# Attention with pooled keys and a mixture of adapters: the second query group by cast and transpose DMAs, and chunks that enter the adapters in another order

## The chip, the cores and the metric

The kernel runs on one core of a Trainium2 chip. The metric is the device time of one execution in microseconds (us). The core's engines work side by side, each through its own instructions in order: TensorE (PE in the profile; its weight loads are PEld), VectorE (DVE), ScalarE (ACT), GpSimd (POOL) and SyncE (SP), which here only issues DMAs. Matmuls write to PSUM[...].

## What is computed

Four batches of 12288 queries of 128 channels attend to 768 keys each. The keys, which are also the values, are the means of 4x4 patches of `kv`, times `w_sr`. Each row of the result then goes through the two best of eight low-rank adapters, weighted by a softmax over the two logits, and is added to itself.

```python
kv_pool = kv.reshape(B, H // r, r, W // r, r, C).mean(axis=(2, 4))
kv_flat = kv_pool.reshape(B, -1, C) @ w_sr
k = v = kv_flat
s = scale * (q @ k.transpose(0, 2, 1))
...
out = (a @ v)                      # a = softmax(s); these are the rows x
...
logits = x @ w_gate                # 8 adapters, the two best are kept
...
z = x[mask] @ A[e]                 # 128 -> 16
delta[mask] += w[mask, k, None] * (z @ B[e])
return (x + delta)
```

## The kernel before

A *chunk* is 512 queries: 24 chunks a batch, 96 in all. Four chunks are a *query group* `g` (2048 queries), whose transposed form `qT[g]` is what the scores need. Nearly all groups are made by two DMAs: a cast to bf16 into DRAM, issued by GpSimd, and a transposing DMA into SBUF, issued by SyncE. The first two groups are instead loaded as f32, transposed on TensorE and copied by ScalarE:

```python
def cast_q(g):
    t = qdram.tile([GT, C], BF16, tag=f"q{g}", name=f"qbf{g}")
    keep(nc.gpsimd.dma_start(t, q[g // NG, (g % NG) * GT:(g % NG + 1) * GT]))
    q_bf[g] = t

def load_qT(g):
    t = qpool.tile([P, GT], BF16, tag="qT", name="qT")
    keep(nc.sync.dma_start(t.rearrange("c (j p) -> c j p", p=P),
                           q_bf[g].rearrange("(p j) c -> p (j c)", p=P), transpose=True))
    qT[g] = t
...
def turn_q(g, m, engine):
    ...
    for i in range(S):
        mm(ps[:, i], q_f[g][:, m * S + i], id_f, is_transpose=True,
           start=(i == 0), stop=(i == S - 1))
    ...
        keep(nc.scalar.copy(o, ps))
...
load_q(0, 0, GC * S)
for h in range(3):
    for r in range(4):
        for x in range(2):
            load_kv(0, h, r, x)
for m in range(GC):
    load_q(1, m * S, m * S + S)
```

The scores of a chunk come in three parts of 256 keys, each two matmuls of 512 columns and one exponential. They share two PSUM buffers. The weighted sum over the values needs 24 matmuls of 137 columns (128 channels, 8 logits of the adapters, and the sum of the weights) into a single PSUM buffer, which `normalize` empties:

```python
def scores(k, r):
    ...
    ps = ps_s.tile([P, 2, T], FP32, tag="sg", name="sg")        # 2 buffers
    for i in range(2):
        mm(ps[:, i], kfT[b][:, 2 * r + i], rhs, start=True, stop=True)
    keep(nc.scalar.activation(em[k][:, 2 * r:2 * r + 2], ps, AF.Exp, bias=0.0, scale=scale))

def normalize(k):
    keep(nc.vector.reciprocal(ri, acc[k][:, :, VC]))
    ...
    keep(nc.vector.tensor_tensor(x, acc[k][:, :, 0:VC],
                                 ri.unsqueeze(2).broadcast_to([P, S, VC]), op=ALU.mult))
```

The adapters of a chunk `k` then take, in later steps: `top` (VectorE finds the sorted logits), `route` (differences, a tanh on ScalarE, the gate weights `gw`; on VectorE for the first groups, on GpSimd for the others), `transposes` (of `x` and of the gated hidden rows `hg`, four matmuls each, with one copy out of PSUM), `down` (x times A), `gate` (VectorE), `up` (times B), and `finish` (the sum with `x` on VectorE, and the output DMA). Chunks are routed in groups of the sizes

```python
sizes = [1, 1, 2] + [GC] * (NCHUNK // GC - 5) + [2] * 4 + [1] * 8
```

The main loop has one step for each `k` from 4 on, and `enter` says which chunks enter the adapters in it (`kx`; `kh` is what entered in the step before, `ku` the one before that). `att` names the chunks whose weighted sum is taken in a step: one, but two in the steps 6, 7 and 8.

```python
late = const.tile([P, 1], FP32)
keep(nc.gpsimd.tensor_copy(late, q_f[1][:, GC * S - 1, 0:1]))
for g in range(2, 4):
    cast_q(g)
...
turn_q(1, 0, nc.scalar)
...
for k in range(NCHUNK):
    done = normed[first[k] + size[k] - 1]
    two = size[k] < GC and k % 4 == 0 and len(enter.get(e, [])) < 2
    e = max(e if two else e + 1, done + 1)
    enter.setdefault(e, []).append(k)
...
for k in range(LA, NCHUNK):
    ...
    scores(k, 0)
    while later:
        later.pop(0)()                  # tanh and gate weights of a route
    for n in kn:
        normalize(n)
    ...
    for x_, h_ in pairs[:1]:
        transposes(x_, h_)
    if k + 1 in range(GC + 1, 2 * GC):
        turn_q(1, (k + 1) % GC, nc.scalar)
    scores(k, 1)
    for u_ in ku:
        up(u_)
        finish(u_)
    ...
    scores(k, 2)
    for x_ in kx[:1]:
        down(x_)
        gate(x_)
    ...
            attend(a_, s)
    for x_, h_ in pairs[1:]:
        transposes(x_, h_)
    for x_ in kx[1:]:
        down(x_)
        gate(x_)
    ku = kh
    kh = kx
    if b + 1 < B and 10 <= i < 21:
        ...                             # GpSimd sums patches of the next batch's keys
```

After the loop a tail, written out by hand, finishes the last four chunks.

Of the kernel before, what the change touches and what calls it, by code (L numbers as in the profile page):

```python
# [10 lines left out]
FP32 = mybir.dt.float32  # L11
# [9 lines left out]
def kernel(  # L21
# [104 lines left out]
    for h in range(3):  # L126
        for r in range(4):
            for x in range(2):
                load_kv(0, h, r, x)
    for m in range(GC):  # L130
        load_q(1, m * S, m * S + S)
    b_f = const.tile([P, C], FP32)
    keep(nc.sync.dma_start(b_f, moe_B.rearrange("e r c -> (e r) c")))
    a_f = const.tile([P, P], FP32)
# [131 lines left out]

    sizes = [1, 1, 2] + [GC] * (NCHUNK // GC - 5) + [2] * 4 + [1] * 8
    first, size = {}, {}  # L270
    for n in sizes:
        k0 = len(first)
# [11 lines left out]

    def route(k0):
        n = size[k0] * S
        eng = nc.gpsimd if k0 > 1 else nc.vector
        lg = xg[k0].rearrange("p m s c -> p (m s) c")[:, 0:n, C:VC]
        so = srt[k0].rearrange("p m s e -> p (m s) e")[:, 0:n]

        def over(i):
            d = rpool.tile([P, GC * S, 8], FP32, tag=f"over{i}", name=f"over{i}")[:, 0:n]
            keep(eng.tensor_tensor(  # L293
                d, lg, so[:, :, i].unsqueeze(2).broadcast_to([P, n, 8]), op=ALU.subtract))
            return d

        arg, mask = over(0), over(1)
        keep(eng.tensor_tensor(arg, arg, mask, op=ALU.add))
        keep(eng.tensor_scalar(mask, mask, 0.0, None, op0=ALU.is_ge))


        def rest():
            gates(k0, n, eng, arg, mask)

        if k0 > 3:
            later.append(rest)
        else:
            rest()
# [6 lines left out]
        keep(eng.tensor_tensor(w[:, 0:n], w[:, 0:n], mask, op=ALU.add))  # L315
        gw[k0] = w

    def transposes(kx, kh):

        ps = mtile([P, 2, S, P], BF16, name="tt_ps")  # L320
        if kx is not None:
            xb = xn[kx].bitcast(U16)[:, :, 1::2].bitcast(BF16)
            for s in range(S):
                mm(ps[:, 0, s], xb[:, s, 0:C], id_bf, is_transpose=True,
                   start=(s == 0), stop=(s == S - 1))
        if kh is not None:
            for s in range(S):
                mm(ps[:, 1, s], hg[kh][:, s], id_bf, is_transpose=True,
                   start=(s == 0), stop=(s == S - 1))
        sb = run.tile([P, 2, S, P], BF16, tag="tts", name="tts")  # L330
        lo = 0 if kx is not None else 1
        hi = 2 if kh is not None else 1
        keep(nc.vector.tensor_copy(sb[:, lo:hi], ps[:, lo:hi]))  # L333
        if kx is not None:
            xT[kx] = sb[:, 0]
        if kh is not None:
            hgT[kh] = sb[:, 1]

    def down(k):
        hp[k] = mtile([P, S, P], name="h_ps")  # L340
        for s in range(S):
            mm(hp[k][:, s], xT[k][:, s], a_bf, start=(s == 0), stop=(s == S - 1))
# [44 lines left out]
    rest = []  # L387

    late = const.tile([P, 1], FP32)
    keep(nc.gpsimd.tensor_copy(late, q_f[1][:, GC * S - 1, 0:1]))  # L390
    for g in range(2, 4):
        cast_q(g)
    a_bf = const.tile([P, P], BF16)
    keep(nc.vector.tensor_scalar(a_bf, a_f, 0.5, None, op0=ALU.mult))
    b_bf = const.tile([P, C], BF16)
    keep(nc.vector.tensor_copy(b_bf, b_f))
    turn_q(1, 0, nc.scalar)


    att = {LA: [0], LA + 1: [1], LA + 2: [2, 3], LA + 3: [4, 5], LA + 4: [6, 7]}  # L400
# [3 lines left out]
    for t, ks in att.items():  # L404
        for k in ks:
            normed[k] = t + 1 if k == ks[-1] else t
    enter = {}
    e = 0
    for k in range(NCHUNK):
        done = normed[first[k] + size[k] - 1]  # L410
        two = size[k] < GC and k % 4 == 0 and len(enter.get(e, [])) < 2
        e = max(e if two else e + 1, done + 1)
        enter.setdefault(e, []).append(k)

    sums, rest = [], []
    kh, ku = [], []
    for k in range(LA, NCHUNK):
        b, i = divmod(k, NB)
        ka = att.get(k, [])
# [5 lines left out]
            if 4 <= g + 2 < B * NG and g + 2 not in q_bf:  # L425
                cast_q(g + 2)
        if b + 1 < B:
            if i == 4:
                sums, rest = prepare(b + 1, nc.gpsimd)
            if 4 <= i < 16:  # L430
                h, j = divmod(i - 4, 4)
                load_kv(b + 1, h, j, None)

        def after_norm(kn):
# [9 lines left out]
        scores(k, 0)  # L444
        while later:
            later.pop(0)()
        for n in kn:
            normalize(n)
        pairs = [(kx[j] if j < len(kx) else None, kh[j] if j < len(kh) else None)
                 for j in range(max(len(kx), len(kh)))]  # L450
        for x_, h_ in pairs[:1]:
            transposes(x_, h_)
        if k + 1 in range(GC + 1, 2 * GC):
            turn_q(1, (k + 1) % GC, nc.scalar)
        scores(k, 1)
        for u_ in ku:
            up(u_)
# [11 lines left out]
        for x_ in kx[:1]:  # L469
            down(x_)  # L470
            gate(x_)
        if rest and i in (14, 15, 16, 18, 19, 20, 21, 22, 23):
            rest.pop(0)()
        for a_ in ka[-1:]:
            for s in range(1 if len(ka) == 1 else 0, S):
                attend(a_, s)
        for x_, h_ in pairs[1:]:
            transposes(x_, h_)
        for x_ in kx[1:]:
            down(x_)  # L480
            gate(x_)
        ku = kh
        kh = kx
        if b + 1 < B and 10 <= i < 21:
            h, j = divmod(i - 10, 4)
            for _ in range((4, 3, 1, 0)[j]):
                sums[h].pop(0)()

    K = NCHUNK - 1
    assert kh == [K - 3] and ku == [K - 4], (kh, ku)  # L490
# [92 lines left out]
    gate_part(K - 2, 0, S)  # L583
    add_there(K - 4)

    ri = rpool.tile([P, S], FP32, tag="rinv", name="rinv")
    keep(nc.vector.reciprocal(ri, o95[:, :, VC]))
    xn[K] = xpool.tile([P, GC, S, VC], FP32, tag="xn", name="xn")[:, 0]
    for s in range(2):
        keep(nc.scalar.activation(xn[K][:, s, 0:C], o95[:, s, 0:C], AF.Copy, bias=0.0,  # L590
                                  scale=ri[:, s:s + 1]))
    lg = rpool.tile([P, S, E], FP32, tag="lg", name="lg")
    keep(nc.vector.tensor_tensor(lg, o95[:, :, C:VC], ri.unsqueeze(2).broadcast_to([P, S, E]),
                                 op=ALU.mult))
    keep(nc.vector.tensor_tensor(xn[K][:, 2:S, 0:C], o95[:, 2:S, 0:C],  # L595
                                 ri[:, 2:S].unsqueeze(2).broadcast_to([P, 2, C]), op=ALU.mult))
    tanhs()
    so = rpool.tile([P, S, 8], FP32, tag="so", name="so")
    for s in range(S):
# [15 lines left out]
    fetch(xT, K)  # L615
    th = rpool.tile([P, S, E], FP32, tag="th1", name="th1")
    keep(nc.scalar.activation(th, arg, AF.Tanh, bias=0.0, scale=0.5))
    gate_part(K - 1, 0, S)
    gw[K] = gpool.tile([P, S, E], FP32, tag="gw1", name="gw1")
    keep(nc.vector.scalar_tensor_tensor(gw[K], th, 1.0, mask, op0=ALU.add, op1=ALU.mult))  # L620
    down_into(K, ps_s)
    fetch(hgT, K - 2)
    carry(K - 3)
    add_there(K - 3)
    gate_part(K, 0, 2)
    gate_part(K, 2, S)
    up_into(K - 2, wide(bank(ps_s)))
    turn_h(K - 1, ps_m)
    fetch(hgT, K - 1)
    ps = bank(ps_m).bitcast(BF16).rearrange("p a b -> p (a b)")[:, 0:T].rearrange("p (s c) -> p s c", s=S)  # L630
    hgT[K] = run.tile([P, S, P], BF16, tag="tt1", name="tt1")
    for lo in (0, 2):
        for s in range(lo, lo + 2):
            mm(ps[:, s], hg[K][:, s], id_bf, is_transpose=True, start=(s == lo), stop=(s == lo + 1))
    keep(nc.scalar.copy(hgT[K][:, 0:2], ps[:, 0:2]))
    add_here(K - 2, 0, S, nc.sync)
    keep(nc.vector.tensor_copy(hgT[K][:, 2:S], ps[:, 2:S]))
    up_into(K - 1, bank(ps_m))
    dp[K] = wide(bank(ps_a))
    for lo in (0, 2):  # L640
        for s in range(lo, lo + 2):
            mm(dp[K][:, s], hgT[K][:, s], b_bf, start=(s == lo), stop=(s == lo + 1))
    add_here(K - 1, 0, S, nc.sync)
    add_here(K, 0, 2, nc.scalar)
    add_here(K, 2, S, nc.sync)


# [28 lines left out]
```

The softmax here doesn't subtract the row's maximum and nothing guards it: scores larger than these inputs give would overflow.

## Time and profile before

| | before |
|---|---|
| time, median of 3 runs | 407.59 us (407.49 to 407.65) |
| span in the profile | 405.0 us |
| PE busy | 383.8 us (95%) |
| DVE busy | 324.9 us (80%) |
| ACT busy | 292.2 us (72%) |
| POOL busy | 170.4 us (42%) |
| DMA moved | 76.45 MB, mean 189 GB/s |
| exponential, 128x1024 | 288 of 1023 ns |
| score matmuls, 512 columns | 576, 170.9 us |
| value matmuls, 137 columns | 2280, 171.6 us |
| qT_ps, f32 transposes | 32, 6.1 us |

The busy share of an engine is its time at work over the span. Slices cut the span into 40 equal parts and give a busy share in tenths, a digit a part. A line of a timeline gives start, length, engine, source line, operation, result and source tiles, and how many; in brackets stands the idle time of that engine just before it and what ended it. Names with an arrow read "result from source": `tt_ps<-id_bf,xn` are the transposes of `x`, `sg` are scores, `acc` are weighted sums.

### The profile page before, as it was taken

The numbers are of one execution on the slowest core, as the hardware profiler recorded it, in microseconds if no ns is written. First come the engines' busy times: TensorE is split into PE (matmuls) and PEld (weight loads), VectorE is DVE, ScalarE is ACT, GpSimd is POOL, SyncE is SP. The second block draws the span as 40 slices with busy tenths as digits, with TensorE's granted clock in tenths as the row PEclk, the third lists the DMA queues.
The fourth block names the chain that finished last, engine by engine and source line by source line (L and its number), as shares of the span: only waits on it lengthen the run. The fifth ranks groups of instructions, "written<-read, shape, count | busy, mean of one in ns | idle before, by whom it ended". The sixth has DMA issues, their size and how long they took to land.

```text
span 405.0 us, 11448 instructions
## 1 busy us (share of the span) xinstructions
PE 383.8 (95%) x4589; PEld 307.4 (76%) x4589; DVE 324.9 (80%) x950; ACT 292.2 (72%) x343; POOL 170.4 (42%) x289
## 2 busy tenths in 40 slices
PE   3898899999999999999999999999999999989893
PEld 3656778888888888888888888888888788777682
DVE  2543778888888888889888888889888888888885
ACT  2489468767678778767678778867678778667683
POOL 0010128778512318779411319779411313114342
PEclk9999999999999999999999999999999999999996
DMA  8997577994855999994844999996855765542213
GB/s 305 382 264 243 125 163 210 299 201 123 183 130 108 298 180 337 290 230 126 183 131 107 304 171 321 216 296 151 187 132 114 172 134 92 143 131 102 83 53 133
DMA packets 71318, 76.45 MB, mean 189 GB/s; under 512 B 49920, under 2 KB 50432, under 8 KB 70784
## 3 DMA queue, kind: packets, MB, share of 16 engines
q1 hardware_dynamic: 70128, 63.98, 55.3%
q0 software_dynamic: 704, 11.54, 16.8%
q8 instruction: 36, 0.59, 0.6%
q10 hardware_dynamic: 432, 0.20, 0.2%
q14 instruction: 18, 0.15, 0.1%
HBM read 50.53 MB, written 36.70 MB: 215 GB/s over the span
## 4 chain that ended last, share of the span: by engine, by line
PE 88%; DVE 5%; ACT 2%; DMA 1%; issue 1%; POOL 0%; DVEq 0%; ACTq 0%
PE acc L68 34%; PE sg L68 28%; PE tt_ps L68 9%; PE h_ps L68 5%; PE d_ps L68 5%; PE kpT_ps L68 2%; ACT em L246 2%; DVE xn L263 1%; DMA w_sr_sb<-in_w_sr_dram 1%; PE qT_ps L68 1%; PE v_ps L68 1%; DVE tts L333 1%; PE kfT_ps L68 1%; DVE hg L347 1%; DVE kvr L175 1%
## 5 line engine op out<-in xcount | busy, mean ns | idle before, releaser
L246 ACT ACTIVATE em<-sg 128x1024 f16<-128x1024 f32 x288 | 278.9, 1023 | 91.6 <-PE sg L68 91.4
L68 PE MATMUL sg<-qT,kfT 128*128 128x512 bf16 x576 | 170.9, 378 | 2.7 <-ACT em L246 2.2
L68 PE MATMUL acc<-vx,em 128*128 128x137 f16 x2280 | 171.6, 224 | 1.7 <-DVE xn L263 1.6
L68 PEld LDWEIGHTS <-em 128*128 128x128 f16 x2304 | 149.6, 98 | 4.0 <-DVE xn L263 2.2
L68 PEld LDWEIGHTS <-tts 128*128 128x128 bf16 x740 | 56.4, 98 | 45.8 <-DVE tts L333 2.1
L293 POOL TENSOR_TENSOR over<-xn,srt 128x128 f32<-128x128 f32 (+2 forms) x62 | 21.4, 363 | 157.2 <-DVE srt L281 157.2
L347 DVE TENSOR_TENSOR hg<-h_ps,gw 128x512 bf16<-128x512 f32 x93 | 64.2, 690 | 13.2 <-POOL gw L315 7.5
L263 DVE TENSOR_TENSOR xn<-acc,rinv 128x544 f32<-128x544 f32 x95 | 68.8, 724 | 3.3
L333 DVE COPY tts<-tt_ps 128x1024 bf16<-128x1024 bf16 (+1 forms) x96 | 64.4, 671 | 3.6 <-PE tt_ps L68 3.6
L171 POOL TENSOR_TENSOR kvr<-kvr 128x512 f32<-128x512 f32 x54 | 66.7, 1270 | 0.0
L360 DVE TENSOR_TENSOR osb<-d_ps,xn 128x512 f32<-128x512 f32 x91 | 62.5, 690 | 0.5 <-PE d_ps L68 0.5
L68 PEld LDWEIGHTS <-kfT 128*128 128x128 bf16 x576 | 45.9, 97 | 6.0 <-issue 3.7
L68 PEld LDWEIGHTS <-xn 128*128 128x128 bf16 x384 | 29.3, 98 | 21.9 <-DVE xn L595 0.5
L258 DVE RECIPROCAL rinv<-acc 128x4 f32<-128x4 f32 x95 | 17.2, 181 | 32.7 <-PE acc L68 31.5
L68 PE MATMUL h_ps<-a_bf,tts 128*128 128x128 bf16 x372 | 36.0, 219 | 1.6 <-DVE tts L333 1.6
L68 PE MATMUL d_ps<-b_bf,tts 128*128 128x128 bf16 x364 | 35.2, 219 | 1.3 <-DVE tts L333 1.3
L68 PE MATMUL tt_ps<-id_bf,xn 128*128 128x128 bf16 x372 | 35.9, 219 | 0.0
L68 PE MATMUL tt_ps<-id_bf,hg 128*128 128x128 bf16 x368 | 35.6, 219 | 0.3 <-DVE hg L347 0.3
L281 DVE MAX8 srt<-xn 128x8 f32<-128x8 f32 x380 | 34.2, 153 | 0.2
L314 POOL TENSOR_TENSOR gw<-th,over 128x128 f32<-128x128 f32 (+2 forms) x31 | 12.0, 387 | 37.1 <-ACT th L312 37.0
L68 PEld LDWEIGHTS <-hg 128*128 128x128 bf16 x384 | 25.4, 98 | 0.7 <-DVE hg L347 0.4
L169 POOL TENSOR_TENSOR kvr<-kvr 128x512 f32<-128x512 f32 (+1 forms) x18 | 18.1, 1004 | 0.9
(83 smaller groups left out, 175.4 us busy)
## 6 DMA issues: line engine op xcount, KB each, us to landing
out_dram<-osb SPq DMA_DIRECT2D x95, 256.0 KB, 3.6
kvr<-in_kv_dram SPq DMA_DIRECT2D x36, 512.0 KB, 6.3
qbf<-in_q_dram POOLq DMA_DIRECT2D x22, 512.0 KB, 6.3
kvr<-in_kv_dram SPq DMA_DIRECT2D x24, 256.0 KB, 4.9
qf<-in_q_dram SPq DMA_DIRECT2D x1, 1024.0 KB, 5.0
qf<-in_q_dram SPq DMA_DIRECT2D x4, 256.0 KB, 5.0
qT<-qbf SPq DMA_TRANSPOSE x22, 6.9
out_dram<-osb ACTq DMA_DIRECT2D x1, 128.0 KB, 3.2
```

The costliest lines, as they stand in the source:

```text
L68: return keep(nc.tensor.matmul(*a, **k))
L169: keep(adder.tensor_tensor(u, u, v, op=ALU.add))
L171: keep(adder.tensor_tensor(u[:, lo:hi], u[:, lo:hi], v[:, lo:hi], op=ALU.add))
L246: keep(nc.scalar.activation(em[k][:, 2 * r:2 * r + 2], ps, AF.Exp, bias=0.0, scale=scale))
L258: keep(nc.vector.reciprocal(ri, acc[k][:, :, VC]))
L263: keep(nc.vector.tensor_tensor(x, acc[k][:, :, 0:VC], ri.unsqueeze(2).broadcast_to([P, S, VC]), op=ALU.mult))
L281: keep(nc.vector.max(srt[k0][:, m, s], xn[k][:, s, C:VC]))
L293: keep(eng.tensor_tensor(d, lg, so[:, :, i].unsqueeze(2).broadcast_to([P, n, 8]), op=ALU.subtract))
L314: keep(eng.tensor_tensor(w[:, 0:n], th, mask, op=ALU.mult))
L333: keep(nc.vector.tensor_copy(sb[:, lo:hi], ps[:, lo:hi]))
L347: keep(nc.vector.tensor_tensor(hg[k].rearrange("p s (e r) -> p (s e) r", e=E), hp[k].rearrange("p s (e r) -> p (s e) r", e=E), gw[k0][:, m ...
L360: keep(nc.vector.tensor_tensor(osb, dp[k], xn[k][:, :, 0:C], op=ALU.add))
```

## The change

The second query group is no longer loaded as f32 and transposed on TensorE. It is cast and transposed by DMA, right behind the loads of the first batch's keys: a tiny GpSimd copy that reads the last key load holds the cast until then, and another that reads `qT[1]` holds the casts of the groups 2 and 3 until the transpose has landed. Beside it come the changes of an earlier form, joined with it: chunks are routed one by one at both ends and in pairs between; the chunk that enters in a step is found by readiness, with two in the steps 73 and 75 only; the second transposes of such a step go to ScalarE for the copy, and their down product into the next step; the key loads and sums of the next batches are spread differently over the steps; and in the tail the last chunk is normalized in one operation and gates, transposes and sums of the last two chunks come in halves.

```diff
-    for m in range(GC):
-        load_q(1, m * S, m * S + S)
...
-    sizes = [1, 1, 2] + [GC] * (NCHUNK // GC - 5) + [2] * 4 + [1] * 8
+    sizes = [1] * GC + [2] * (NB * (B - 1) // 2 - 2) + [1] * NB
...
-        eng = nc.gpsimd if k0 > 1 else nc.vector
+        eng = nc.gpsimd if k0 >= GC else nc.vector
...
+        if engine is nc.scalar:
+            keep(nc.scalar.copy(sb[:, lo:hi], ps[:, lo:hi]))
+        else:
+            keep(nc.vector.tensor_copy(sb[:, lo:hi], ps[:, lo:hi]))
...
-    keep(nc.gpsimd.tensor_copy(late, q_f[1][:, GC * S - 1, 0:1]))
+    keep(nc.gpsimd.tensor_copy(late, kvr[0, 2][:, 3, 1, 0:1]))
+    cast_q(1)
+    load_qT(1)
+    late2 = const.tile([P, 1], BF16)
+    keep(nc.gpsimd.tensor_copy(late2, qT[1][:, GT - 1:GT]))
     for g in range(2, 4):
         cast_q(g)
...
-    turn_q(1, 0, nc.scalar)
...
+    ready = {k: normed[first[k] + size[k] - 1] + (k >= GC or k == 2) for k in range(NCHUNK)}
+    enter, t, left = {}, LA, list(range(NCHUNK - 3))
+    while left:
+        can = [k for k in left if ready[k] <= t]
+        enter[t] = can[:2] if t in (NB * (B - 1) + 1, NB * (B - 1) + 3) else can[:1]
+        left = [k for k in left if k not in enter[t]]
+        t += 1
...
-            if i == 4:
+            i0 = 4 if b == 0 else 0
+            if i == i0:
                 sums, rest = prepare(b + 1, nc.gpsimd)
...
+        for x_ in kd:
+            down(x_)
...
-            transposes(x_, h_)
-        if k + 1 in range(GC + 1, 2 * GC):
-            turn_q(1, (k + 1) % GC, nc.scalar)
+            transposes(x_, h_, nc.vector)
+        for x_ in kd:
+            gate(x_)
...
+                if s == S - 1:
+                    for x_, h_ in pairs[1:]:
+                        transposes(x_, h_, nc.scalar)
+                        kd = [x_] if x_ is not None else []
                 attend(a_, s)
...
-        kh = kx
-        if b + 1 < B and 10 <= i < 21:
-            h, j = divmod(i - 10, 4)
-            for _ in range((4, 3, 1, 0)[j]):
-                sums[h].pop(0)()
+        kh = kx[:1] + kdone
+        kdone = kd
+        if b + 1 < B and i % 2 == 0 and (8 if b == 0 else 6) <= i <= 20:
+            for _ in range(4 if b == 0 and i % 4 else 3):
+                sums.pop(0)()
...
-    for s in range(2):
-        keep(nc.scalar.activation(xn[K][:, s, 0:C], o95[:, s, 0:C], AF.Copy, bias=0.0,
-                                  scale=ri[:, s:s + 1]))
...
+    acc[K] = o95
+    normalize(K)
+    lg = xn[K][:, :, C:VC]
...
-    gate_part(K, 0, 2)
-    gate_part(K, 2, S)
+    halves = [(K, 0), (K, 2), (K - 1, 0), (K - 1, 2)]
+    for k, lo in halves:
+        gate_part(k, lo, lo + 2)
```

## The prediction

> **What bounds the kernel now.** I read the page from the top: busy shares, the slices, the chain of waits; then busy time by stretch, which tells where TensorE is not full; then the timeline of the two stretches that stood out.
>
> The slices:
>
> ```profile
> PE   3898899999999999999999999999999999989893
> ACT  2489468767678778767678778867678778667683
> DMA  8997577994855999994844999996855765542213
> ```
>
> TensorE is at 9 nearly everywhere; neither ACT nor the DMA engines stay at their top. The chain of waits is 88% PE. So a gain can only come from TensorE work that disappears, or from the places where TensorE waits. Busy time by stretch finds those (columns: length, then PE, PEld, DVE, ACT, POOL):
>
> ```profile
> 30.00:42.00 12.00, 10.61 (x111) 7.89 (x108) 4.38 (x17) 10.25 (x14) 0.00 (x0) 1.00 0.82 236
> 42.00:54.00 12.00, 10.91 (x136) 8.66 (x136) 8.60 (x35) 6.20 (x9) 2.43 (x7) 1.00 0.59 123
> ...
> 110.00:130.00 20.00, 20.00 (x251) 15.98 (x249) 17.44 (x51) 15.22 (x17) 3.21 (x7) 1.00 0.70 143
> ...
> 330.00:350.00 20.00, 19.48 (x244) 15.56 (x242) 16.62 (x48) 15.11 (x18) 6.34 (x17) 1.00 0.62 143
> 350.00:370.00 20.00, 18.30 (x231) 14.57 (x228) 16.92 (x50) 13.68 (x18) 4.50 (x15) 1.00 0.34 97
> 370.00:384.00 14.00, 12.89 (x165) 10.35 (x163) 11.61 (x32) 9.58 (x13) 4.85 (x21) 1.00 0.24 90
> ```
>
> From 70 to 330 us TensorE is full, and a step of the main loop takes 3.68 us (in the chain its 18 value matmuls start at 120.30, 123.98, 127.66). It idles before 6 us, about 2.5 us in 30 to 54, 0.52 + 1.70 + 1.11 = 3.3 us in 330 to 384, and after 392. The change touches the last three.
>
> The start, where the second query group is made (timeline; start, length):
>
> ```profile
> 25.16 1.26 POOL L79 DMA_DIRECT2D qbf<-in_q_dram  x2
> ...
> 28.98 0.59 PE L68 MATMUL sg<-qT,kfT 128*128 128x512 bf16 x2 [0.33 <-ACT em L246]
> ...
> 29.41 0.60 PE L68 MATMUL qT_ps<-id_f,qf 128*128 128x128 f32 x4
> ...
> 29.84 1.66 PE L68 MATMUL acc<-vx,em 128*128 128x137 f16 x24
> ...
> 30.80 2.45 SPq L84 DMA_TRANSPOSE qT<-qbf  x1
> 31.33 0.59 PE L68 MATMUL sg<-qT,kfT 128*128 128x512 bf16 x2
> ```
>
> 31.33 is the first score of chunk 4, the first to use the second query group. DMA issues in the windows 25.1 to 25.6 and 30.5 to 31 show how long such a cast and such a transpose take when little else runs (5.6 and 4.6 us to landing):
>
> ```profile
> qbf<-in_q_dram POOLq DMA_DIRECT2D x1, 512.0 KB, 5.6
> qT<-qbf SPq DMA_TRANSPOSE x1, 4.6
> ```
>
> The late stretch, one step in which a second chunk enters the adapter:
>
> ```profile
> 347.39 0.39 PE L68 MATMUL tt_ps<-id_bf,xn 128*128 128x128 bf16 x4
> ...
> 347.82 0.42 DVE L333 COPY tts<-tt_ps 128x512 bf16<-128x512 bf16 x1 [0.65 <-PE tt_ps L68]
> ...
> 348.30 0.40 PE L68 MATMUL h_ps<-a_bf,tts 128*128 128x128 bf16 x4 [0.52 <-DVE tts L333]
> ```
>
> TensorE transposes the second chunk, has nothing else in its order, and waits for VectorE's copy.
>
> **What the skill says.** "DMA: Bandwidth & Descriptors", section "SWDGE vs HWDGE vs iDMA": a cast in flight must be issued from GpSimd and a transpose from SP or ACT, so the new path is two DMAs, the second waiting for the first. The trace agrees: the cast issued at 25.16 lands 5.6 us later, at 30.8, where the transpose starts. "PSUM — Partial Sum Buffer", section "Engine vs sequencer instructions": ACT, VectorE and GpSimd queues are strict FIFO and matmuls stay in program order; the wait at 348.30 is such a case, and I use it to follow the new order. "TensorE: Matmul & The Clock Gate", section "Back-to-back issue gap": N/2.4 + 2.5 ns a matmul. A steady step has 6 of 512, 24 of 137 and 16 of 128 columns, 8408 columns and 46 matmuls: estimate 3.62 us, measured 3.68, so I count 0.438 ns a column. "SBUF — State Buffer", section "SBUF: two separate sides": a GpSimd operation that reads SBUF is locked out while VectorE adds two SBUF inputs; VectorE does that from 21.19 to 23.67, so the new gate may start a few tenths late. No number here shows that yet.
>
> **Part by part.**
>
> (1) *Second query group.* Removed: four loads of 256 KB, 16 f32 transposes on TensorE (about 0.5 us per four in the stream, 2.0 us) and four ACT copies of 0.6 us. Added: gate, cast, transpose in series. The old gate fired at 25.04, when the query loads behind the keys had landed. In the DMA packets, the last key packet ends about 3 us before the last query packet, near 22.0. With 0.1 to 0.6 us for gate and issue: cast from about 22.4, landed 28.0, transposed 32.6. TensorE would be ready about 30.75 (31.33 less 0.5 for the absent transposes). So a new wait of about 1.9 us; chunk 4 starts at 32.6 instead of 31.33, 1.3 us later. The third group (cast at 32.8, landed about 38.4, transposed by 43 to 48) is needed only about 20 us after chunk 4, near 52: hidden.
>
> (2) *The first five steps.* Before, chunk 4 to chunk 9 takes 31.33 to 55.95, 24.6 us. The new order makes the first four chunks groups of one, routed on VectorE, and each enters one step earlier, so one chunk more of adapter work (4 x 512 = 2048 columns, 0.9 us) is done by chunk 9. Columns: 5x3072 + 7x3288 + 3584 + 2048 + 1024 = 45032, 19.7 us if full. Waits, with the durations of the page (exponential 0.96 to 1.02, normalize 0.9, route about 1.07 plus gate weights 0.4, gate 0.69): in steps 4 and 5 TensorE runs two PSUM buffers ahead of ACT at most, +1.7; in step 6 VectorE routes chunk 2 and then chunk 1 before it gates chunk 1 (about 3.8 us from the normalize), and the next hidden transpose waits for it, +1.4; in step 7 normalize, route and gate of chunk 3 cost +2.1; step 8, +1.0. Sum 25.9 us, 1.3 more than before. Chunk 9 then starts at 58.5, 2.6 us later.
>
> (3) *Late doubles.* Before, chunks enter six steps behind at first and three at the end: three double steps. From the score starts 343.71, 348.53, 352.76, 357.25 one double takes 4.82 + 4.23 + 4.49 = 13.54 instead of 3x3.68 = 11.04: 2.5 us, of which 0.9 is its work. Three: 7.5 us. After: five steps behind, so two doubles (steps 73 and 75), the second transpose copied by ACT inside the value matmuls and its down product put into the next step. Each keeps 0.9 us of work; for waits I leave 0.7 in all, mostly step 76 where VectorE has two gates and two sums, 3.33 + 1.38 = 4.7 against 4.1 us of TensorE. Two: 2.5 us. Saved 5.0. (This includes the one chunk done earlier in part 2.)
>
> (4) *Middle.* Groups of two instead of four: more small GpSimd operations, TensorE's order per step unchanged: 0 expected.
>
> (5) *Tail.* Before, the last score step ends near 391.6 and the program at 405.0, 13.4 us. Normalizing the last chunk in one VectorE operation lets its transposes go at about 395.2 instead of 395.7; gates and sums come in halves, and the last sums, now ending at 400.70, end about 0.5 earlier. Saved 0.5.
>
> Sum: +2.6 - 5.0 - 0.5 = -2.9; 407.6 - 2.9 = 404.7, rounded to 404.8.
>
> **Rivals.** (A) *The DMA pair takes the place of the transposes and more*: for it, 5.6 + 4.6 us in series and median landings of 6.3 and 6.9 over the whole run; against it, the DMA engines are nearly free then. With the medians chunk 4 starts at about 35.5 and the total is near 407.7. (B) *ACT and VectorE become the bound in the middle*: 34 pairs bring more tanhs, and an ACT held up by a late GpSimd result holds the scores. For it: 3 or 4 key sums of 1.27 us sit before the route on GpSimd; three end about 2.7 us into the odd step, where the logits arrive at 2.8, four end at 3.9 and leave only a tenth before the tanh. Against: ACT is 75 to 80% busy. 0.1 us a pair would be 3.5 us, total about 408. (C) *My waits in the first steps are too high*: ACT loses 2.4 us of copies where it is the bound, and then the start costs nothing: total near 402.5.
>
> **Range and chances.** About 1 us each for the landing, the early waits and the doubles, and a one-sided 1 to 3 us for (B): 402.2 to 408.2. Two per cent is 8.1 us; faster by that means 399.4, more than all TensorE idle that the change can reach in (2), (3) and (5) together. Faster 0.04, same 0.94, slower 0.02.
>
> **What would show it.** A TensorE wait on the DMA transpose near 31 to 33 us of 1 to 3 us; chunk 9 at about 58.5; 20.00 of 20.00 TensorE busy in the middle (less would be rival B); under 1.2 us of idle between 330 and the tail; the last sum 12.9 us or less after the last score step. I am wrong if the query transpose lands before 31 or after 35, if the middle step is not 3.68, or if the doubles still wait for a copy.

## The result, and the profile after

The changed kernel takes 413.31 us (median of four, 410.96 to 422.76) against 407.54 us for the kernel before on the same chip. The ratio is 1.0123, with a 95% interval of 1.008 to 1.0166: a loss of 5 to 6 us in 407 where a gain of 2.9 was forecast, outside the range. The same kernel once more gave 412.5 us and 1.0119 (1.0087 to 1.0151). The first execution profiled took 422.76 us and holds a wait of its own, shown further down, so the profile after is here that of an execution of 409.57 us, the shortest of the eight, span 407.6 against 405.0.

Its page, the slices and the chain of waits:

```profile
PE   3896798999999999999999999999999999999992
...
DMA  8959883992739999987767997862862736653213
...
PE 82%; DMA 6%; DVE 4%; SPq 3%; ACT 2%; POOL 1%; issue 1%; DVEq 0%; ACTq 0%
```

The 8s that stood near the end of TensorE's row are now 9: the late idle is gone, as intended. But the row is lower in slices 4 to 7 (6, 7, 9, 8), about 30 to 70 us. DMA, 1% of the chain before, is 6%.

Busy time by stretch, the same stretches as in the prediction (length, then PE, PEld, DVE, ACT, POOL, clock, DMA share, GB/s):

```profile
30.00:42.00 12.00, 8.35 (x82) 5.46 (x81) 4.30 (x17) 8.26 (x10) 1.57 (x4) 1.00 0.87 175
42.00:54.00 12.00, 9.49 (x127) 7.93 (x125) 9.21 (x43) 4.69 (x8) 0.00 (x0) 1.00 0.92 251
110.00:130.00 20.00, 20.00 (x252) 16.37 (x249) 17.67 (x55) 15.32 (x20) 6.25 (x20) 1.00 0.67 159
330.00:350.00 20.00, 20.00 (x255) 16.31 (x254) 17.02 (x52) 15.88 (x21) 8.95 (x36) 1.00 0.51 144
350.00:370.00 20.00, 20.00 (x251) 16.10 (x250) 17.37 (x49) 16.06 (x23) 8.01 (x32) 1.00 0.69 149
370.00:384.00 14.00, 14.00 (x178) 11.28 (x176) 11.93 (x36) 11.16 (x15) 5.99 (x24) 1.00 0.20 76
```

TensorE idles 3.65 + 2.51 = 6.2 us between 30 and 54, where it idled 2.5. The middle is full, and so is everything from 330 to 384. The loss must lie before 70 us, or in places that these stretches leave out.

The start (timeline: start, length):

```profile
23.01 0.28 POOL L391 COPY late<-kvr 128x1 f32<-128x1 f32 x1 [21.70 <-DMA kvr<-in_kv_dram]
23.23 0.76 POOL L79 DMA_DIRECT2D qbf<-in_q_dram  x1
...
29.02 2.53 SPq L84 DMA_TRANSPOSE qT<-qbf  x1
...
30.17 1.66 PE L68 MATMUL acc<-vx,em 128*128 128x137 f16 x24
...
33.62 1.04 PE L68 MATMUL sg<-qT,kfT 128*128 128x512 bf16 x4 [1.79 <-DMA qT<-qbf]
33.63 0.18 POOL L395 COPY late<-qT 128x1 bf16<-128x1 bf16 x1 [9.65 <-DMA qT<-qbf]
```

Gate at 23.01, cast landed where the transpose starts (29.02), transpose landed at 33.6. TensorE ends its last ready work at 31.83 and waits 1.79 us. Chunk 4 starts at 33.6 instead of 31.3.

I then cut each trace at the first score weight load of a step and took the differences. "Start" is the start of chunk 4, "end" runs from the score start of step 95 to the end of the span; all in us:

| | start | steps 4 to 8 | 9 and 10 | 11 to 71 | 72 to 81 | 82 to 94 | end | span |
|---|---|---|---|---|---|---|---|---|
| before | 31.27 | 24.61 | 7.36 | 232.57 | 36.80 | 55.34 | 17.08 | 405.0 |
| after | 33.61 | 26.42 | 8.91 | 232.62 | 40.79 | 47.84 | 17.40 | 407.6 |
| difference | +2.34 | +1.81 | +1.55 | +0.05 | +3.99 | -7.50 | +0.32 | +2.6 |

This table locates all of the 2.6 us. Two columns were not in the forecast at all (9 and 10, and the sign of the end). It does not yet tell why the other seven executions take 1.4 to 13.2 us more than this one.

### The profile page after: what moved, and what is told of

It is laid out like the page before. It is cut to its first block, busy times and chain, and to the rows that moved or that the text cites. A ratio compares the mean times of both kernels' runs of the same rounds, so it can differ in the third digit from the quotient of the medians.

```text
span 420.7 us, 11578 instructions
## 1 busy us (share of the span) xinstructions
PE 380.1 (90%) x4500; PEld 306.1 (73%) x4573; DVE 327.2 (78%) x957; ACT 295.4 (70%) x370; POOL 197.9 (47%) x447
## 4 chain that ended last, share of the span: by engine, by line
PE 69%; DMA 18%; DVE 5%; SPq 2%; issue 2%; POOL 1%; ACT 1%; DVEq 0%; POOLq 0%; ACTq 0%
PE acc L68 27%; PE sg L68 20%; DMA qT<-qbf 14%; PE tt_ps L68 9%; PE d_ps L68 5%; PE h_ps L68 5%; SPq L98 2%; DMA qbf<-in_q_dram 2%; DMA qf<-in_q_dram 1%; DMA kvr<-in_kv_dram 1%; DVE xn L261 1%; DVE rinv L256 1%; PE v_ps L68 1%; POOL kvr L169 1%; DVE hg L348 1%
## 5 line engine op out<-in xcount | busy, mean ns | idle before, releaser
L68 PE MATMUL sg<-qT,kfT 128*128 128x512 bf16 x503 | 156.9, 383 | 15.0 <-DMA qT<-qbf 13.0
L334 DVE COPY tts<-tt_ps 128x1024 bf16<-128x1024 bf16 (+1 forms) x91 | 62.6, 688 | 18.9 <-PE tt_ps L68 18.9
L291 POOL TENSOR_TENSOR over<-xn,srt 128x64 f32<-128x64 f32 (+1 forms) x114 | 29.7, 281 | 80.6 <-DVE srt L279 80.4
L312 POOL TENSOR_TENSOR gw<-th,over 128x64 f32<-128x64 f32 (+1 forms) x57 | 16.6, 291 | 87.1 <-ACT th L310 87.0
L297 POOL TENSOR_SCALAR over<-over 128x64 f32<-128x64 f32 (+1 forms) x57 | 19.0, 333 | 5.1
```

The lines of the kernel that those rows point to most:

```text
L68: return keep(nc.tensor.matmul(*a, **k))
L291: keep(eng.tensor_tensor(d, lg, so[:, :, i].unsqueeze(2).broadcast_to([P, n, 8]), op=ALU.subtract))
L312: keep(eng.tensor_tensor(w[:, 0:n], th, mask, op=ALU.mult))
```

## The experiments

The first theory after the result (theory T in the expectations) was that the transposes of the query pair land late and that this is what costs. Its rival (M) was that the new order of chunks is slow by itself. The first four experiments showed a part of each and two things more, a stall in step 10 and a spread of the times. For the spread, theory C names the casts that are issued right behind transposes, and rival L the first cast and transpose alone. All experiments are compared with the kernel before on the same chip (407.64 to 407.84 us); intervals are 95%.

### The same kernel again

No edit.

> The changed kernel once more, unchanged, to get a second profile. Theory T (the query transposes by DMA land late): the time is again 411 to 414 us and TensorE again waits 2 to 4 us for the first DMA transpose near 31 to 35 us; the 9 us wait for a transpose near 273 us was one bad landing, and is shorter or gone here. Rival M (the middle itself became slower through the pairs on GpSimd): TensorE shows less than 19.8 of 20 us in most stretches from 70 to 330 us, without any wait on a DMA.

Measured: 412.5 us (409.57 to 420.8), ratio 1.0119 (1.0087 to 1.0151). The loss repeats and so does the spread, of more than 10 us, where the kernel before keeps within 1.3 us. The trace shown above is from here. In its step 10 stands this (timeline):

```profile
60.79 3.72 POOL L169 TENSOR_TENSOR kvr<-kvr 128x512 f32<-128x512 f32 x3
...
64.48 0.31 POOL L312 TENSOR_TENSOR gw<-th,over 128x64 f32<-128x64 f32 x1
...
64.86 0.32 POOL L313 TENSOR_TENSOR gw<-gw,over 128x64 f32<-128x64 f32 x1
...
65.22 0.69 DVE L348 TENSOR_TENSOR hg<-h_ps,gw 128x512 bf16<-128x512 f32 x1 [2.42 <-POOL gw L313]
...
65.97 0.40 PE L68 MATMUL tt_ps<-id_bf,hg 128*128 128x128 bf16 x4 [1.38 <-DVE hg L348]
```

GpSimd sums three patches of the next keys (3.72 us), and only then makes the gate weights of the first pair, whose tanh was ready at 61.95. VectorE waits 2.42 us for them, TensorE 1.38 for VectorE. Step 10 takes 5.23 us instead of 3.68: the +1.55 of the table. It happens once, because the first pair's gate weights fall due in the step after these sums; from step 11 on the two orders run alike.

### The query pair alone, on the kernel before

```diff
-    for m in range(GC):
-        load_q(1, m * S, m * S + S)
...
-    keep(nc.gpsimd.tensor_copy(late, q_f[1][:, GC * S - 1, 0:1]))
+    keep(nc.gpsimd.tensor_copy(late, kvr[0, 2][:, 3, 1, 0:1]))
+    cast_q(1)
+    load_qT(1)
+    late2 = const.tile([P, 1], BF16)
+    keep(nc.gpsimd.tensor_copy(late2, qT[1][:, GT - 1:GT]))
...
-    turn_q(1, 0, nc.scalar)
...
-        if k + 1 in range(GC + 1, 2 * GC):
-            turn_q(1, (k + 1) % GC, nc.scalar)
```

> The kernel before with the second query group alone by cast and transpose DMA (gates included), everything else as before. Theory T: the wait for the transpose costs about 3 us at 31 to 35 us, the slow clock after it 1 to 2 us more, less 2 us of transposes that are gone and up to 2.4 us of ACT copies: 408.5 to 411 us. Rival M (the joined scheduling is what costs): 407 us or less.

Measured: 411.32 us (410.91 to 411.85), ratio 1.0091 (1.0076 to 1.0106), that is +3.7 us from this part alone. Its trace (timeline):

```profile
23.30 0.76 POOL L79 DMA_DIRECT2D qbf<-in_q_dram  x1
...
30.28 2.47 SPq L84 DMA_TRANSPOSE qT<-qbf  x1
...
35.02 1.46 PE L68 MATMUL sg<-qT,kfT 128*128 128x512 bf16 x3 [3.72 <-DMA qT<-qbf]
```

The cast is issued as in the trace above, but lands 6.98 us later instead of 5.79; TensorE waits 3.72 us and chunk 4 starts at 35.0, 3.74 us later than before. Nearly all of the loss is there. Steps 4 to 8 give back only 0.13, with TensorE at half clock from 34.69 to 38.10. So the query pair is not innocent.

### The new order alone: query group 1 loaded as f32 and transposed on TensorE

```diff
-    keep(nc.gpsimd.tensor_copy(late, kvr[0, 2][:, 3, 1, 0:1]))
-    cast_q(1)
-    load_qT(1)
-    ...                                # late2 too
+    keep(nc.gpsimd.tensor_copy(late, q_f[1][:, GC * S - 1, 0:1]))
...                                     # load_q(1, ...) and turn_q(1, ...) as in the kernel before
```

> The changed kernel with the second query group loaded as f32 and transposed on TensorE as before, the joined scheduling kept. Theory T: 403.5 to 406 us, as the late double steps are cheaper and the long wait at 31 to 35 us is gone. Rival M: 408 us or more, with transposes still landing late in the middle.

Measured: 408.01 us (20 executions, 407.47 to 415.09), ratio 1.0029 (1.0007 to 1.005). The new order is worth nothing by itself, and the 403.5 to 406 us of theory T did not come: by the table's cuts +3.34 in steps 4 to 8, +1.55 in 9 and 10, -3.51 from 72 to 94, and the end 0.8 shorter. Thirteen executions lie below 409.5 us and seven between 409.83 and 415.09. This spread comes without the query pair, so something else in the new order makes it.

Against this kernel the changed one has 2.34 us more at the start and 26.42 instead of 27.95 in steps 4 to 8. The 16 transposes and four copies that the query pair takes away are thus worth 1.5 us in those steps, and their replacement costs more.

### The cast at the very start

```diff
     load_q(0, 0, GC * S)
+    cast_q(1)
...
     keep(nc.gpsimd.tensor_copy(late, kvr[0, 2][:, 3, 1, 0:1]))
-    cast_q(1)
```

> The changed kernel with the cast of the second group issued at the very start, beside the first loads, and its transpose in the SyncE queue behind the key loads; the casts of the groups 2 and 3 held as in the change. The cast then competes with the keys (1.5 MB more traffic in the first 20 us), which should delay the keys by up to 4 us, but the transpose can start at about 19 to 23 us and land before 30. Theory T: no wait for the transpose, total between 404 and 409 us, depending on the keys' delay. Rival M: no better than the changed kernel, 410 us or more.

Measured: 409.07 us (408.19 to 416.57, 12 executions), ratio 1.0045 (1.0025 to 1.0065), some 3 us better than the changed kernel. The queries have landed by 27.15 and TensorE never waits for them. Yet chunk 4 starts at 32.85, 1.6 us after the kernel before: the cast now shares the DMA engines with the key loads, and VectorE makes the first keys' `kfT` at 16.59 and the last keys' at 27.65, against 14.97 and 25.64 in the kernel before and 15.91 and 26.40 in the changed one. Early or late, those bytes cost the start something.

### Later casts one step later, with either way for the queries

In the changed kernel, a transpose is issued in the steps where `k % 4` is 0 and the next group's cast follows 1.0 to 2.1 us behind it. In the kernel before, the casts come 5 to 11 us behind (five pairs from 112 to 193 us). The edit moves it by a step, once in the changed kernel and once in the one with TensorE transposes:

```diff
-            if 4 <= g + 2 < B * NG and g + 2 not in q_bf:
-                cast_q(g + 2)
+        if k % GC == 1 and 4 <= k // GC + 2 < B * NG:
+            cast_q(k // GC + 2)
```

> The changed kernel with the casts of the later query groups issued one step after the transposes instead of in the same step (steps 9, 13, 17 and so on instead of 8, 12, 16). Theory C (the spread of the changed kernel, 409.6 to 414 us and more, comes from each cast starting about 1.2 us after a transpose on the same 16 DMA engines, so that some transposes land after the chunk that needs them): the spread falls to 1 to 2 us and the median to 409.5 to 411 us, with the first wait near 31 to 35 us left. Rival L (the spread comes from the first cast and transpose alone): the median stays at 412 us.

> The same edit on the joined form with the second query group transposed on TensorE, which had 407.5 to 415.1 us in 20 runs, seven of them over 409.5. Theory C: all runs within 407.2 to 408.5 us. Rival L: as there is no first cast to wait for, the seven late runs cannot be its doing, so under L nothing changes and about a third of the runs stay over 409.5.

Measured: 413.1 us (412.17 to 415.1), ratio 1.0138 (1.0114 to 1.0162), with the query pair; 409.86 us (409.6 to 409.95), ratio 1.0051 (1.0038 to 1.0063), with TensorE's transposes. The median gets 1.9 us worse in the second, but the spread is gone: five executions within 0.35 us. With the query pair 3 us of spread stay, and the median is not the 409.5 to 411 us that theory C expected. In its trace, of 415.1 us, chunk 4 starts at 35.1, half clock follows from 36.1 to 42.9 and again from 70.2 to 73.6, and steps 9 and 10 take 11.16 us. So both theories hold a part there. Landing times of the transposes between 60 and 380 us (the view of the line that issues them), first for the kernel with TensorE's transposes, then for the same with the casts a step later:

```profile
DMA to landing us min/median/max: 4.4/8.3/9.3
```

```profile
DMA to landing us min/median/max: 4.5/5.8/11.7
```

The typical landing falls from 8.3 to 5.8 us, and so it is in every trace of the new order: 8.3 to 9.2 in the four with the old place, 5.4 to 5.8 in the eight with the new one (medians). The longest one does not fall here, 11.7 against 9.3. What a late one does is shown only by the 422.76 us execution of the changed kernel (timeline, and the DMA engines' busy tenths from 260 to 282 us):

```profile
256.82 8.76 SPq L84 DMA_TRANSPOSE qT<-qbf  x1
...
258.07 0.58 POOL L79 DMA_DIRECT2D qbf<-in_q_dram  x1
...
282.36 1.04 PE L68 MATMUL sg<-qT,kfT 128*128 128x512 bf16 x2 [8.99 <-DMA qT<-qbf]
```

```profile
DMA  9999900000900099000920099008090499943000
```

The transpose takes 25.5 us to land and TensorE waits 9 us. The DMA engines are not full: they stand idle between bursts. So it is not a lack of bandwidth; what the transpose and the cast wait for in these gaps the trace does not name.

Why the median rises is plain in the trace. The cast of step 9 now stands on GpSimd before the same gate weights, VectorE waits 3.0 instead of 2.4 us, and TensorE's clock falls to half for exactly 3.4 us. The stretch 67.0 to 70.4 with the casts later, and the same stretch without:

```profile
67.00:70.40 3.40, 3.40 (x28) 2.85 (x26) 1.75 (x7) 1.71 (x2) 3.40 (x4) 0.50 0.44 92
```

```profile
67.00:70.40 3.40, 3.40 (x47) 2.81 (x45) 2.99 (x10) 2.65 (x4) 3.32 (x4) 1.00 0.50 148
```

28 matmuls begin instead of 47 with TensorE busy throughout. Steps 9 and 10 take 11.07 us instead of 8.91: 0.6 from the later gate, the rest at half clock.

### The new order mended

Three edits on the last kernel (TensorE's transposes, casts a step later): chunks 2 and 3 are routed on GpSimd, with tanh and gate weights put off to the next step like those of later chunks; no key sum comes before the first pair's gate weights; the doubles stand at steps 73 and 77 instead of 73 and 75. The changed line for `ready` moves no chunk: chunk 2 takes step 7, so chunk 3 enters in step 8 with either line.

```diff
-        eng = nc.gpsimd if k0 >= GC else nc.vector
+        eng = nc.gpsimd if k0 > 1 else nc.vector
...
-    ready = {k: normed[first[k] + size[k] - 1] + (k >= GC or k == 2) for k in range(NCHUNK)}
+    ready = {k: normed[first[k] + size[k] - 1] + (k >= 2) for k in range(NCHUNK)}
...
-        enter[t] = can[:2] if t in (NB * (B - 1) + 1, NB * (B - 1) + 3) else can[:1]
+        enter[t] = can[:2] if t in (NB * (B - 1) + 1, NB * (B - 1) + 5) else can[:1]
...
-        if b + 1 < B and i % 2 == 0 and (8 if b == 0 else 6) <= i <= 20:
-            for _ in range(4 if b == 0 and i % 4 else 3):
+        n_add = ((1 if 9 <= i <= 19 else 0) if i % 2 else (3 if 10 <= i <= 20 else 0)) if b == 0 else (
+            3 if i % 2 == 0 and 6 <= i <= 20 else 0)
+        if b + 1 < B:
+            for _ in range(n_add):
                 sums.pop(0)()
```

> The joined form with the second query group on TensorE, the casts one step later, and three of its own stalls taken out: no key sums before the gate weights of the first pair (step 10 took 5.23 us instead of 3.68), chunks 2 and 3 routed on GpSimd as before (steps 6 and 7 took 7.30 and 7.71 us against 5.72 and 6.13), and the two double steps at 73 and 77 instead of 73 and 75 (step 76 took 5.49 us). If these stalls are what ate the gain of the joined form: step 10 at 3.7, steps 6 and 7 together 2 us shorter, doubles 1 to 1.5 us shorter, sum about 4.5 us: 403 to 404.5 us. If VectorE or GpSimd only passes the wait on: 406 us or more.

Measured: 404.26 us (403.76 to 404.31), ratio 0.9912 (0.9898 to 0.9925). It beats both kernels, by 3.6 and by 8 to 9 us. The wait in the step that took 5.23 us is gone (timeline, step 10):

```profile
58.48 0.58 POOL L79 DMA_DIRECT2D qbf<-in_q_dram  x1
...
59.93 0.32 POOL L314 TENSOR_TENSOR gw<-th,over 128x64 f32<-128x64 f32 x1 [0.88 <-ACT th L312]
60.32 0.32 POOL L315 TENSOR_TENSOR gw<-gw,over 128x64 f32<-128x64 f32 x1
...
60.75 0.69 DVE L350 TENSOR_TENSOR hg<-h_ps,gw 128x512 bf16<-128x512 f32 x1
```

GpSimd now waits for the tanh, not the other way round, and VectorE has no bracket before its gate. Steps 9 and 10 take 7.36 us again, as before: 3.71 of the 5.4 us between this trace and the last. Steps 4 to 8 take 26.31 instead of 27.95, with the same matmuls in them, and of the edits only the routing reaches that far: step 7 takes 6.49 instead of 7.71, step 8 5.73 instead of 6.15. Step 6 stays at 7.30, against 5.73 in the kernel before, though less was expected. The late doubles take 3.53 more than single steps instead of 3.99, a smaller gain than the 1 to 1.5 us expected. The transposes land in 5.6 us (median, at most 7.1).

### The mended order with the tail of before

```diff
-    acc[K] = o95
-    normalize(K)
-    ...                                # gates, transposes and sums of the last two chunks in halves
+    ...                                # the tail of the kernel before
```

> The same with the tail of the kernel before. The new tail ended its last sum 13.0 to 13.2 us after the last score step began, the old one 12.7: if that holds, 0.3 to 0.5 us less than the mended kernel; if the two tails are equal or the new one wins, the same or up to 0.5 us more.

Measured: 404.9 us (404.57 to 405.43), ratio 0.9931 (0.9917 to 0.9944), 0.64 us above the new tail. In the traces the new tail's last sum ends 0.7 us later after the start of step 95 (13.3 against 12.6), and the program ends 0.95 us sooner after it (3.02 against 3.97). But the profile of the old tail's kernel also has its chunk 4 start 0.6 us later, at 32.14, and it keeps the full clock to the end of its last sum, where the new tail is at half clock from 10.4 us after the start of step 95. So this is no clean measure of the tail: it gains at most 0.6 us, and not in the way I had worked out.

### The mended order with the query pair

The edit of the second experiment on the mended kernel.

> The mended kernel (404.26 us) with the second query group by cast and transpose DMA as in the change: the query part of the change alone, on a base without the other stalls. Theory T (landing): the first score of chunk 4 starts at 33.6 to 35.2 us instead of 31.5, and where TensorE idles over 3 us it runs at half clock for the next 3.4 us: 2 to 4 us from the wait, up to 1.9 from the clock, less about 1.5 us for the absent transposes and copies: 405.5 to 409 us. Rival: the query part costs little by itself, and in the changed kernel it was the meeting with other stalls that hurt: 404.5 to 405 us.

Measured: 408.15 us (407.33 to 408.7, 13 executions), ratio 1.0009 (1.0001 to 1.0017): 3.9 us lost against the mended kernel (4.05 with each set against the kernel before on its own chip), as it lost 3.7 on the kernel before. Chunk 4 starts at 34.55, after a wait of 3.54 us, and then the clock drops (by stretches of 1 us; the number before the last two is the clock):

```profile
35.00:36.00 1.00, 0.58 (x3) 0.19 (x2) 0.00 (x0) 0.81 (x1) 0.66 (x2) 0.99 1.81 295
36.00:37.00 1.00, 0.73 (x2) 0.25 (x2) 0.00 (x0) 1.00 (x2) 0.00 (x0) 0.50 1.32 229
37.00:38.00 1.00, 1.00 (x4) 0.26 (x3) 0.00 (x0) 0.81 (x2) 0.00 (x0) 0.50 0.00 0
38.00:39.00 1.00, 1.00 (x7) 0.71 (x6) 0.34 (x2) 1.00 (x2) 0.00 (x0) 0.50 0.31 66
39.00:40.00 1.00, 1.00 (x10) 0.61 (x8) 0.90 (x9) 0.74 (x2) 0.00 (x0) 0.80 2.20 459
```

The wait is paid twice: once while TensorE stands, and again in the 3.4 us (36.0 to 39.4) in which it runs at half clock.

### The same, with idle work on TensorE in the wait

```diff
+            idle = mtile([P, S, P], name="idle_ps")
+            for s in range(24):
+                mm(idle[:, s % S], id_f, id_f, is_transpose=True, start=True, stop=True)
             ka = []
```

Nothing reads the result; it only keeps TensorE at work for most of the wait.

> The same, with 24 f32 transposes of the identity into an unread PSUM tile in the wait, about 3 us of TensorE work that serves nothing. Theory T with the clock as a part of the cost: no half clock after the wait, and 1 to 2 us less than without them whenever the landing is late, the spread under 1.5 us. If the clock has no part: the same time as without them or up to 0.5 us more.

Measured: 406.58 us (406.33 to 407.12), ratio 0.9972 (0.9961 to 0.9984), 1.6 us better for work that does nothing. Chunk 4 starts at 34.73, no earlier. Two stretches of its trace:

```profile
34.00:36.00 2.00, 1.04 (x4) 0.41 (x5) 0.00 (x0) 0.63 (x1) 1.10 (x3) 1.00 0.07 14
36.00:38.00 2.00, 1.23 (x8) 0.59 (x8) 0.00 (x0) 2.00 (x3) 0.00 (x0) 1.00 1.52 262
```

The clock stays at 1.00. The two traced executions differ by 1.0 us. Steps 4 to 8 take 24.79 instead of 25.44 us, which is 0.65 of it; another 0.6 lies between the last sum and the end of the program, which I cannot tie to the clock. The mean granted clock over the span agrees in the executions that were not traced: 0.992 to 0.996 in all six here, 0.983 to 0.991 in the thirteen without the idle work.

### The same, without the hold on the next casts

```diff
-    late2 = const.tile([P, 1], BF16)
-    keep(nc.gpsimd.tensor_copy(late2, qT[1][:, GT - 1:GT]))
```

> The same as e9 without the hold on the casts of the groups 2 and 3, which then follow the first cast at once. If the hold is worth something, the transpose shares the DMA engines with two casts of 1.5 MB of traffic each and lands 2 to 6 us later: 408 to 413 us. If not, as e9.

Measured: 409.93 us (409.56 to 411.01), ratio 1.0061 (1.0044 to 1.0078), 1.8 us worse than with the hold. The transpose is issued at 29.83 but lands at 36.95, in 7.1 instead of 4.6 us, with the other two casts beside it. The hold, then, does what it was put there for.

### The same, released by the second third of the keys

```diff
-    keep(nc.gpsimd.tensor_copy(late, kvr[0, 2][:, 3, 1, 0:1]))
+    keep(nc.gpsimd.tensor_copy(late, kvr[0, 1][:, 3, 1, 0:1]))
```

> The same as e9 with the cast released by the second third of the keys instead of the last (about 6 us earlier). The last third of the keys then shares the DMA engines with the cast and comes up to 3 us later, but the transpose can start near 24 us and land near 29: first score of chunk 4 at 31.5 to 33 us, 404.5 to 406 us, if the keys lose less than the queries win; otherwise as e9.

Measured: 405.44 us (405.36 to 406.84), ratio 0.995 (0.9934 to 0.9967), 2.7 us better than the later release. The cast goes out at 18.16 and the queries have landed at 31.66; TensorE no longer waits for them. But the keys and queries share the DMA engines, the last keys' `kfT` is made at 28.34 instead of 25.59, the chunks before the fourth run later, and chunk 4 starts at 33.54. It stays 1.2 us above TensorE's own transposes.

## Why the prediction was wrong

By its own terms, against the execution of 409.57 us (us; the prediction's part 3 and its share in the sum are what it called late doubles):

| term | predicted | measured |
|---|---|---|
| (1) start of chunk 4 | +1.3 | +2.34 |
| (2) steps 4 to 8 | +1.3 | +1.81 |
| (4) middle, which holds step 10 | 0 | +1.60 |
| (3) late doubles | -5.0 | -3.51 |
| (5) tail | -0.5 | +0.32 |
| sum | -2.9 | +2.6 |

The misses are 1.0, 0.5, 1.6, 1.5 and 0.8 us; no single one carries the result. (407.6 less 2.9 is 404.7; the 404.8 on record is a slip of 0.1.)

**(1) The query pair.** The step that failed is "cast from about 22.4, landed 28.0, transposed 32.6". The cast was issued at 23.2 in place of 22.4 (the gate's copy of one column took 0.28 to 0.68 us beside VectorE's key sums, against 0.18 for the one from `qT[1]` later on: the few tenths that the prediction had allowed for). The cast took 5.8 us here, near the 5.6 of before, but 6.7 to 7.1 in five other traces with this gate and hold. So chunk 4 started at 33.6 to 35.1. Rival (A) named this, at 35.5, and I gave it too little weight because "the DMA engines are nearly free then": I took a single duration at its lowest, although the page gave a median of 6.3. "TensorE would be ready about 30.75" (31.33 less 0.5 is 30.83) was late too, at 31.83, since the keys landed later in this execution. What I had left out altogether is the price after the wait: in each trace with a wait of 3.26 us or more for this transpose TensorE was at half clock, for 3.4 or 6.8 us. The Trainium skill, "TensorE: Matmul & The Clock Gate", section "HAM oscillation — how this bites in real kernels", warns of exactly this, a wait for a DMA after which the work starts cold; I had read the page for its column cost alone. The traces agree, with 0.50 granted from 36.0 to 39.4 in the mended kernel with the query pair. The execution of the table, with 1.79 us of wait, kept the full clock.

The saving, four times 0.5 us, was right where it can be read: 1.5 us for three of them in steps 4 to 8, as the two ways with the same order show (27.95 against 26.42). The query pair loses in each of the four kernels in which both ways were run (3.7 on the kernel before, 4.5 on the new order, 3.2 with the casts a step later, 3.9 on the mended one, with the saving already in it).

**(2) The first steps.** 25.9 us forecast, 26.42 measured, in part by luck: the waits were put at 6.2 us and TensorE stands 5.0 there, but it is busy 21.4 us where 19.7 was worked out from the columns. And with TensorE's transposes the same order takes 27.95 there, 3.3 us more than before. Routing four chunks on VectorE in a stage where it also normalizes and gates is half of that: the mended kernel, with two of the four on GpSimd, has 26.31 with the transposes in. Most of the other half is step 6.

**(4) The middle.** "TensorE's order per step unchanged: 0 expected" failed in one step of sixty: step 10, +1.55. Rival (B) had the engine and the sums, but put the wait before the tanh, on ScalarE, and at a tenth in each of 34 pairs. That is not there (232.62 against 232.57). The tanh was in time, and the 1.55 is a single wait for the gate weights after it. I followed the order of TensorE's queue through the first steps, and not that of GpSimd's, where the gate weights stand behind 3.72 us of sums.

**(3) The late doubles.** The three doubles of before were worth 7.50 us, as forecast. The two new ones cost 3.99 instead of 2.5, and the step that failed is "for waits I leave 0.7 in all". Step 76 alone takes 5.49 us where I had 4.7. Its start in the profile after (timeline):

```profile
318.68 0.40 PE L68 MATMUL h_ps<-a_bf,tts 128*128 128x128 bf16 x4 [0.30 <-ACT tts L332]
...
319.57 0.69 DVE L334 COPY tts<-tt_ps 128x1024 bf16<-128x1024 bf16 x1 [0.64 <-PE tt_ps L68]
...
320.31 0.38 PE L68 MATMUL d_ps<-b_bf,tts 128*128 128x128 bf16 x4 [0.35 <-DVE tts L334]
...
320.91 0.38 PE L68 MATMUL d_ps<-b_bf,tts 128*128 128x128 bf16 x4 [0.21 <-DVE hg L348]
...
321.50 0.59 PE L68 MATMUL sg<-qT,kfT 128*128 128x512 bf16 x2
```

I had counted VectorE's work, 4.7 us, as if it were the bound. But TensorE waits at three places in turn: the deferred down product for ScalarE's copy (0.30), the first up product for VectorE's copy (0.35), the second for VectorE's gate (0.21). Each is work in series on two engines, which a sum for each engine doesn't show. Doubles four steps apart (73 and 77) cost 3.53.

**(5) The tail.** The halves were to end the last sums 0.5 earlier. From step 95 to the end of the last sum it takes 13.1 us instead of 12.75. The transposes of the last chunk were to move from 7.8 us after the start of step 95 to 7.3, and they did. The step that failed is "gates and sums come in halves". The end of the last sums in the profile after (timeline):

```profile
402.08 0.41 DVE L555 TENSOR_TENSOR osb<-tail_ps,xn 128x256 f32<-128x256 f32 x1
...
402.55 0.27 PE L68 MATMUL tail_ps<-b_bf,tt 128*128 128x128 bf16 x2 [0.81 <-DVE osb L555]
402.86 0.42 DVE L555 TENSOR_TENSOR osb<-tail_ps,xn 128x256 f32<-128x256 f32 x1 [0.36 <-PE tail_ps L68]
```

The second half of the last up product, whose operand was ready at 402.04, waits until VectorE has summed the first half out of the same PSUM tile, and the second sum waits for it in turn. The wait is in all eleven traces with the new tail, at 0.60 to 0.81 us. That a tile for each half would remove it is not shown. What follows the last sum varies between traces (4.30 here, 3.02 to 3.10 with the new tail and TensorE's transposes, 4.33 in the kernel before). Why is open.

**What no term held.** The executions of the changed kernel run from 409.57 to 422.76 us. Two causes of the difference are shown: a later landing of the first queries, with half clock behind it (chunk 4 at 34.6 and half clock from 36.1 to 39.5 in the second trace), and transposes in the middle that land late. That putting the casts a step later cures the second is supported by counts with TensorE's transposes, 7 of 20 executions above 409.5 us with the old place and none in 14 with the new off the median of its own kernel by more than 0.6 us. The old place and the new ran on different chips, though the kernel before took 407.64 and 407.84 us on the two. The 9 us wait itself was traced once. The terms above explain the execution of 409.57 us. The medians, 412.5 and 413.31, lie 3 to 4 us higher, and how the two causes share that was not measured.

**What held.** The middle step is 3.68 us, TensorE is full from 330 us on, the doubles of before were sized right, and the change stays within 2%. Of the three signs of being wrong, one came: the doubles still wait for a copy. The landing, at 33.6 and 34.6 in the two traces of the changed kernel, lies later than the 32.6 of the sum but inside the 31 to 35 that I had allowed, so that sign was set too wide.

## What to carry to other kernels

Compare a transfer with the work it replaces on the path that sets the end: here 16 transposes worth 2 us on TensorE were cheaper than two DMAs in series that cost it nothing but a wait, and a wait of over 3 us was paid again in a slower clock. When a reorder is laid out, follow each queue in order, GpSimd's also, through the first step in which a new kind of work meets an old one; the steady step tells nothing of it. Take landing times as a spread, not as the best one seen. When work is split into halves, see whether the second half must wait until the first has been read.

## What the runs showed of the hardware

**The clock fell without a full idle window.** Before the tail, half clock always lasted 3.4 or 6.8 us. In the 3.4 us ahead of it TensorE was little busy, though seldom idle: 1.04 us in the mended kernel with the query pair, 1.04 in the second trace of the changed kernel, 1.21 without the hold, 1.43 in the kernel with the casts a step later (63.6 to 67.0, no single wait over 2 us), 0.01 in the query pair alone. The Trainium skill, "TensorE: Matmul & The Clock Gate", section "What's actually happening", gives a window of about 3.4 us and has the clock drop after an idle one. The length agrees, but the window did not have to be idle here. No busy share parts the two outcomes: 3.4 us with 1.62 us busy (31.05 to 34.46 in the profile after) kept the full clock, and 3.4 us with 2.29 (394.9 to 398.3, in the tail of the kernel before) were followed by half clock. What decides in between these traces do not show. The f32 transposes that nothing reads did keep the clock: they are 2.79 us of the wait, from 31.08 to 33.87.

**A transpose landed later when a cast was issued 1 to 2 us behind it.** With 1.0 to 2.1 us between them a transpose landed after 8.3 us (median), with a step more after 5.8, and once after 25.5, with the DMA engines idle in half of the slices shown.

**What follows the last sum is not constant.** Between the end of the last sum and the end of the program lie 3.02 to 3.10 us in the three kernels with the new tail and TensorE's transposes, and 3.4 to 4.3 in those with the new tail and the query pair, though the last sums and their output DMAs are the same.
